# When the v of a later batch is issued, in a linear attention with routed experts behind it

## The chip, the cores and the metric

The kernel runs on one core of a Trainium2 chip. The metric is the device time of one execution in microseconds; lower is better.

## The reference

The inputs q, k and v have the shape (8 batches, 8 heads, 576 tokens, 64), all float32. The first stage is a linear attention, the second a layer of eight experts (512 to 1024 to 512, relu between them) in which a hash of the token's id names its one expert.

```python
q_s = softmax(q, axis=-1); k_s = softmax(k, axis=2)    # over features; over tokens
kv  = einsum('bhsd,bhse->bhde', k_s, v)
x   = einsum('bhsd,bhde->bhse', q_s, kv)               # then (B*S, H*D) = (4608, 512)
e   = token_ids * 2654435761 % 8
out = relu(x @ w1[e]) @ w2[e]                          # each row with its own expert
```

All of k and all of v of a batch must be there before the 64 by 64 matrices `kv` of that batch are complete.

## The kernel before

The program is written engine by engine. A small class, `Emit`, keeps a list of instructions for each engine, and in each list they run in the order in which the Python code emits them. It also works out the waits: an operation names the buffers that it reads (`R`), writes (`W`) and partly writes (`P`), and gets a wait on the semaphore of each engine or transfer that touched them before. The second argument of `em.dma` is the name of the semaphore, the first the engine on whose list the issue stands.

The attention runs over the batches b = 0 to 7, with p = b % 2 as the side of the double buffers. What one batch does:

- q and k (1.18 MB each) come from the SyncE queue, by `load_one` (L290) into `qf[p]` and `kf[p]`. `load(b + 2, p)` (L752) is emitted two batches ahead; the issue of q waits for `exp_q` of batch b (it reads the buffer), that of k for `exp_k` of batch b.
- v comes from the GpSimd queue, by `load_v` (L302), and is turned into bf16 on the way. It has four slots, `vx`, so it can be asked for early.
- ScalarE takes exponentials: `exp_k` (L517, to `ek`) and `exp_q` in two halves (L513, to `eq`).
- TensorE transposes q (`transpose_q`), and `kv(p, n)` (L542) multiplies `ek` with slot n of v: 36 matmuls at L550. `qsum` and `attend` then give the rows `xn`, by VectorE at L582.
- `sort` (L597) brings the rows of the batch before into the order of their experts by a matmul with one-hot columns (L601); ScalarE copies the result to `xs` (L608).
- `segments` (L634) copies pieces of `xs` into `xT`, the experts' input. It is a generator of 16 copies per batch (L645), eight for each of the two groups of tokens, at positions that `load_segments` has put in registers. In most batches GpSimd makes them. `run(gen, n)` (L730) takes the next n of them.

In the loop, TensorE's list for batch b is: transposes of b, first `sort` of b - 1, `kv` of b, second `sort` of b - 1, `qsum`, `attend`. ScalarE's is: `exp_k` of b, a copy of the transposed q, two copies of each `sort` to `xs`, then `exp_q` of b + 1. GpSimd's is: the issue of a v, then the copies of the segments of b - 1, which wait for both pairs of `xs`. So on GpSimd an issue of v written ahead of the copies runs as soon as the copies of the batch before are done.

The order of v before the change, in these lines: v of batches 0 and 1 at the start, of 2 in b = 0, of 3 to 6 in b = 1 to 4, and of 7 in b = 6.

```python
exp_k(p)                      # L744
transpose_q(p)
one_hot(b)
if b > 0:
    sort(1 - p, 0, 3)
...
kv(p, b % 4)                  # L753
if 0 < b < B - 1:
    sort(1 - p, 2, 0)
```

After the loop the experts follow. `l1` (matmuls at L683) and `layer2` (L708) take one expert after the other. Their weights come by the GpSimd queue, the first of them in b = 6 after the v of batch 7, into the memory that q and k leave. The rows are stored by indirect transfers (L724).

Of the kernel before, what the change touches and what calls it, by code (L numbers as in the profile page):

```python
# [164 lines left out]
def fused_kernel(nc, q, k, v, moe_token_ids, moe_w1, moe_w2, out):  # L165
    B, H, S, DH = q.shape
    NTOK = moe_token_ids.shape[0]
    E, D, F = moe_w1.shape
# [119 lines left out]
    b_q, b_k = [Buf(), Buf()], [Buf(), Buf()]  # L288
# [13 lines left out]
    def load_v(b, n, R=()):  # L302
        o = 3 * (n % 2)
        em.dma("pool", "d_v%d" % n, lambda e: e.dma_start(
            vx[n // 2][:, o:o + 2, :, :, :].rearrange("p a j c d -> p (a j) (c d)"),
            v[b].rearrange("(a h) (p c) d -> (h p) a (c d)", h=2, p=64)), R=R, W=[b_vx[n]])
# [24 lines left out]
    for h in range(2):  # L331
        for a in range(2):
# [8 lines left out]
       R=[b_tok], P=[b_ei])  # L341
# [9 lines left out]
       R=[b_ef2, bc["iota8"]], W=[b_flg])  # L351
# [5 lines left out]
          R=[b_flg, bc["upper"], bc["ones"]], W=[bk[6], bk[7]])  # L357
# [13 lines left out]
       R=[b_pr], W=[b_pos])  # L371
# [137 lines left out]
    def load(b, p):  # L509
        load_one("d_q%d", qf, q, b, p, b_q)  # L510
        load_one("d_k%d", kf, k, b, p, b_k)

    def exp_q(p, j):  # L513
        ac(lambda e: e.activation(eq[p][:, j, :, :, :].rearrange("p c a d -> p a c d"),  # L514
                                  qf[p][:, j::2, :, :], ACTF.Exp), R=[b_q[p]], W=[b_eq[p][j]])

    def exp_k(p):  # L517
        ac(lambda e: e.activation(ek[p][:].rearrange("p j c a d -> p a (j c) d"),  # L518
                                  kf[p][:].rearrange("p (a j) c d -> p a (j c) d", a=2), ACTF.Exp),
           R=[b_k[p]], W=[b_ek[p]])  # L520

    def transpose_q(p):

        def tr(e, j, c, o):
            return e.transpose(PBH[:, o:o + 128], eq[p][:, j, c, :, :].rearrange("p a d -> p (a d)"), ident[:])  # L525
        for j in range(2):
            em.op("pe", [lambda e, j=j, c=c: tr(e, j, c, 1024 * j + 128 * c) for c in range(8)],
                  R=[b_eq[p][j], bc["ident"]], W=[bk[j]])
        em.op("pe", [lambda e, j=j: tr(e, j, 8, 2048 + 128 * j) for j in range(2)], R=b_eq[p] + [bc["ident"]],
              W=[bk[2]])  # L530
        for j in range(2):
            o = qT[p][:, j, :, 0:512].rearrange("p h (c x) -> p h c x", x=64)
            i = PBH[:, 1024 * j:1024 * j + 1024].rearrange("p (c h x) -> p h c x", h=2, x=64)
            if j == 0:
                dv(lambda e, o=o, i=i: e.tensor_copy(out=o, in_=i), R=[bk[0]], W=[b_qT[p][0]])
            else:
                ac(lambda e, o=o, i=i: e.activation(o, i, ACTF.Copy), R=[bk[1]], W=[b_qT[p][1]])  # L537
        dv(lambda e: e.tensor_copy(out=qT[p][:, :, :, 512:576],
                                   in_=PBH[:, 2048:2304].rearrange("p (j h x) -> p j h x", h=2, x=64)),
           R=[bk[2]], W=[b_qT[p][2]])  # L540
# [27 lines left out]
    def qsum(p):  # L568
        em.op("pe", [lambda e, t=t, j=j, h2=h2: e.matmul(
            PB[:, 5, 8 * t + 4 * j + 2 * h2:8 * t + 4 * j + 2 * h2 + 2], qt(p, t, j, h2), pair1[:],  # L570
            start=True, stop=True) for t in range(T) for j in range(2) for h2 in range(2)],
            R=b_qT[p] + [bc["pair1"]], W=[bk[5]])
        dv(lambda e: e.reciprocal(out=rq[p][:].rearrange("p t g -> p (t g)"), in_=PB[:, 5, 0:8 * T]), R=[bk[5]],
           W=[b_rq[p]])
# [13 lines left out]
    def one_hot(b):  # L588
        p = b % 2
        for t in range(T):  # L590
            g, i = t // TG, t % TG
            dv(lambda e, g=g, i=i: e.tensor_scalar(  # L592
                out=oneh[p][g][:, i, :], in0=col16[:, 0:GW[g]], scalar1=pos[:, 2 * b + g, i:i + 1],
                scalar2=None, op0=ALU.is_equal),
               R=[b_pos, bc["col16"]], W=([b_oh[p][g]] if i == 0 else ()), P=(() if i == 0 else [b_oh[p][g]]))

    def sort(p, c0, bank):  # L597

        for g, bs in ((0, bk[bank:bank + 2]), (1, bk[bank + 2:bank + 3])):
            n = 3 - g  # L600
            em.op("pe", [lambda e, g=g, i=i, k=k, n=n: e.matmul(  # L601
                PB[:, bank + (k if g == 0 else 2), (0 if g == 0 else GW[1] * k):(GW[0] if g == 0 else GW[1] * (k + 1))],
                xn[p][:, 3 * g + i, 128 * (c0 + k):128 * (c0 + k) + 128], oneh[p][g][:, i, :],
                start=(i == 0), stop=(i == n - 1)) for k in range(2) for i in range(n)],
                R=b_xn[p][3 * g:3 * g + n] + [b_oh[p][g]], W=bs)
            src = PB[:, bank:bank + 2, 0:GW[0]] if g == 0 else \
                PB[:, bank + 2, 0:2 * GW[1]].rearrange("p (k x) -> p k x", k=2)
            ac(lambda e, g=g, src=src: e.activation(xs[p][:, c0:c0 + 2, XO[g]:XO[g] + GW[g]], src, ACTF.Copy),  # L608
               R=bs, P=b_xs[p][c0:c0 + 2])
# [24 lines left out]
    def segments(b, key="pool", half=None):  # L634
        p = b % 2
        for g in range(2):
            for ee in range(E) if half is None else range(4 * half, 4 * half + 4):
                def seg(e, ee=ee, g=g):
                    if half is None:
                        rs, o = regs[key, None, 0], 2 * E * g + 8 * (ee // 4) + ee % 4  # L640
                    else:
                        rs, o = regs[key, half, p], 8 * g + ee % 4
                    so = e.snap(rs[o], min_val=0, max_val=GW[g])  # L643
                    do = e.snap(rs[o + 4], min_val=CAPS * ee, max_val=CAPS * ee + CAP)
                    return e.tensor_copy(out=xT[:, :, bass.ds(do, SEG[g])],  # L645
                                         in_=xs[p][:, :, XO[g]:XO[g] + GW[g] + SEG[g]][:, :, bass.ds(so, SEG[g])])
                em.op(key, seg, R=b_xs[p] + ([] if b < B - 2 else [b_x5[ee]]), W=[(b_x5 if b < B - 2 else b_x7)[ee]])
                yield
# [9 lines left out]
    def weights1(ee, s, R=()):  # L658
        for a in range(2):
            em.dma("pool", "d_w1_%d" % s, lambda e, a=a: e.dma_start(  # L660
                w1b[s][64 * a:64 * a + 64, :, :],
                moe_w1[ee].rearrange("(a g p) f -> a p g f", a=2, g=4)[a]), R=R,
                W=(b_w1[s] if a == 0 else ()), P=(() if a == 0 else b_w1[s]))
# [66 lines left out]
    def run(gen, n=2 * E):  # L730
        for _ in range(n):
            if next(gen, 0) == 0:
                break
# [7 lines left out]
    for b in range(B):  # L741
        p = b % 2
        last = b == B - 1
# [5 lines that stand above are left out]
        if last:  # L749
            sort(1 - p, 2, 0)  # L750
        if b + 2 < B:
            load(b + 2, p)  # L752
# [3 lines that stand above are left out]
        if not last:  # L756
            exp_q(1 - p, 0)
            exp_q(1 - p, 1)
        qsum(p)
        if b == 0:  # L760
            load_v(2, 2)
        elif b < B - 3:
            load_v(b + 2, (b + 2) % 4)
        elif b == B - 2:
            load_v(B - 1, 3)
        if b == B - 2:
            for s, bs in enumerate(([b_q[0], b_k[0]], [b_q[1], b_k[1]])):
                b_w1[s], b_w2[s] = [Buf(*bs), Buf(*bs)], Buf(*bs)
            weights1_half(0, 0, 0)
            weights1_half(0, 0, 1)  # L770
            load_segments(b - 1, "pool")
            run(segments(b - 1))
        elif last:
            weights1(1, 1)
            weights2(0, 0)
            for x in (b - 1, b):
                load_segments(x, "pool", 1)
                load_segments(x, "dve", 0)
            run(segments(b - 1, "pool", 1))
        elif b > 0:  # L780
            load_segments(b - 1, "pool")
            run(segments(b - 1))
        attend(p, 0, 2, 3)
        attend(p, 2, 2, 6)
        attend(p, 4, 1, 5)
        if b == 0:
            segment_table()
            widths()
        if b == 1:
            overflow()  # L790
        if b == 2:
            load_widths()
# [121 lines left out]
    for b in range(B):  # L914
# [11 lines left out]
        for ch in range(4):  # L926
# [4 lines left out]
                R=b_xn[0] + [b_id], W=bk[u:u + 2])  # L931
            ac(lambda e, ch=ch, u=u: e.activation(xg[:, ch, :].rearrange("p (h x) -> p h x", h=2),
                                                  PB[:, u:u + 2, 0:H2], ACTF.Copy), R=bk[u:u + 2], W=[b_xg[ch]])
        for ee in range(E):
# [5 lines left out]
            for t in range(T):  # L940
                u = layer2(NW, t, 2)
                m = flg[:, 2 * b + t // TG, ee, t % TG:t % TG + 1]
                if ee == 0:
                    dv(lambda e, t=t, u=u, m=m: e.tensor_scalar(out=yg[:, t, :], in0=PB[:, u, :], scalar1=m,
                                                                scalar2=None, op0=ALU.mult),
                       R=[bk[u], b_flg], W=[b_yg[t]])
                else:
                    dv(lambda e, t=t, u=u, m=m: e.scalar_tensor_tensor(
                        out=yg[:, t, :], in0=PB[:, u, :], scalar=m, in1=yg[:, t, :], op0=ALU.mult, op1=ALU.add),
                       R=[bk[u], b_flg], W=[b_yg[t]])  # L950
# [39 lines left out]
```

The softmax here doesn't subtract the row's maximum and nothing guards it: scores larger than these inputs give would overflow.

## Time and profile before

| | |
|---|---|
| time | 230.05 us (median of 3 runs, 229.86 to 230.22) |
| span in the profile | 228.4 us |
| TensorE matmuls busy | 198.9 us, 87% |
| GpSimd busy | 121.6 us, 53% |
| VectorE busy | 116.1 us, 51% |
| ScalarE busy | 105.7 us, 46% |
| hardware queue (q, k) | 18.91 MB, 22.9% of the 16 DMA engines' time |
| software queue (v, weights, stores) | 30.94 MB, 67.1% |

Busy time of an engine is the sum over its instructions, and the share is of the whole span. The span falls into two parts. In the first 90 us the attention runs, with all engines busy for part of the time; from there on TensorE works on the experts almost without a pause. An average over both tells little of either, so what the change may do has to be read from the first part. In the views, a line such as L304 is a line of the kernel, and "vx<-in_v_dram" is the transfer from v in the chip's memory to the tile `vx`.

### The profile page before, as it was taken

To read this page: it belongs to the slowest core of one execution; us is meant where nothing else is said; L and a number is where in the kernel's file an instruction comes from. 1 tells how busy PE (TensorE), PEld (TensorE's weight loads), DVE (VectorE), ACT (ScalarE), POOL (GpSimd) and SP (SyncE) were. 2 spreads that over 40 slices of the span, in tenths; PEclk is the share of its full clock that TensorE was granted. 3 is DMA by queue.
4 is the path that set the end of the run, shared out by engine and by line. 5 is a ranking of instruction groups with operands and counts; after the bars stand their busy time and mean duration, and the time that the engine had idled before them with its cause. 6 is when DMAs were issued, how large, how long until landed. Compare 5 with 4: busy or idle time off the path is not lost.

```text
span 228.4 us, 4640 instructions
## 1 busy us (share of the span) xinstructions
PE 198.9 (87%) x1786; PEld 134.5 (59%) x1788; DVE 116.1 (51%) x265; ACT 105.7 (46%) x133; POOL 121.6 (53%) x235
## 2 busy tenths in 40 slices
PE   0459968876899788999999999999999999999990
PEld 0348757654776564775574764754855845845640
DVE  1678798782778867699941322322421422412220
ACT  3385588756888944765342331331422322322311
POOL 8740778773659993670007975805715615125053
PEclk9999999997999999999999999999999999999999
DMA  6999999999996999799993799999999798113023
GB/s 208 295 371 293 292 372 316 301 312 351 297 401 250 149 196 195 119 153 204 207 177 139 160 204 205 330 272 201 290 200 242 163 203 224 73 46 139 24 102 123
DMA packets 29776, 50.25 MB, mean 220 GB/s; under 512 B 2351, under 2 KB 15663, under 8 KB 29744
## 3 DMA queue, kind: packets, MB, share of 16 engines
q0 software_dynamic: 20768, 30.94, 67.1%
q1 hardware_dynamic: 8976, 18.91, 22.9%
q8 instruction: 16, 0.26, 0.4%
q14 instruction: 16, 0.13, 0.2%
HBM read 61.90 MB, written 10.49 MB: 317 GB/s over the span
## 4 chain that ended last, share of the span: by engine, by line
PE 62%; DMA 20%; POOL 6%; ACT 5%; issue 4%; POOLq 1%; DVE 1%; SPq 1%; DVEq 0%; ACTq 0%
PE ps L708 29%; PE ps L683 27%; DMA kf<-in_k_dram 20%; POOL xT L645 4%; PE ps L601 3%; ACT ek L518 3%; PE ps L550 2%; ACT eq L514 1%; POOL out_dram L724 1%; ACT xs L608 1%; PE ps L819 1%; DVE xn L582 1%; POOLq L643 1%; POOL w1b L668 0%; POOL w1b L660 0%
## 5 line engine op out<-in xcount | busy, mean ns | idle before, releaser
L724 POOL DMA_INDIRECT out_dram<-yo,idx x40 | 39.5, 987 | 71.6 <-ACT yo L718 31.8
L708 PE MATMUL ps<-w2b,hT 128*128 128x512 bf16 x320 | 70.4, 379 | 0.0
L683 PE MATMUL ps<-xT,w1b 128*128 128x320 bf16 (+1 forms) x512 | 64.4, 286 | 0.8 <-ACT hT L690 0.8
L683 PEld LDWEIGHTS ps<-xT,w1b 128*128 128x128 bf16 x512 | 49.7, 98 | 15.1 <-ACT hT L690 1.1
L708 PEld LDWEIGHTS ps<-w2b,hT 128*128 128x128 bf16 x320 | 31.2, 98 | 36.3
L645 POOL COPY xT<-xs x112 | 39.6, 412 | 19.4 <-ACT xs L608 17.9
L690 ACT ACTIVATE hT<-ps 128x640 bf16<-128x640 f32 x41 | 28.8, 703 | 39.4 <-PE ps L683 39.0
L718 ACT ACTIVATE yo<-ps 128x512 f32<-128x512 f32 x26 | 15.5, 597 | 54.1 <-PE ps L708 54.1
L692 DVE TENSOR_SCALAR hT<-ps 128x640 bf16<-128x640 f32 x23 | 19.0, 825 | 30.2 <-PE ps L683 30.2
L720 DVE COPY yo<-ps 128x512 f32<-128x512 f32 x14 | 9.7, 692 | 44.0 <-PE ps L708 44.0
L601 PE MATMUL ps<-oneh,xn 128*128 128x384 bf16 (+1 forms) x160 | 25.0, 307 | 1.3 <-ACT qT L537 1.0
L582 DVE TENSOR_TENSOR xn<-ps,rq 128x1024 bf16<-128x1024 f32 (+1 forms) x24 | 23.6, 1041 | 3.2 <-PE ps L577 2.6
L608 ACT ACTIVATE xs<-ps 128x768 bf16<-128x768 f32 (+1 forms) x32 | 19.1, 651 | 9.2 <-PE ps L601 9.1
L518 ACT ACTIVATE ek<-kf 128x2304 bf16<-128x2304 f32 x8 | 17.0, 2123 | 9.9 <-DMA kf<-in_k_dram 9.9
L550 PE MATMUL ps<-vx,ek 64*128 64x192 bf16 x288 | 15.2, 264 | 7.2 <-ACT ek L518 7.2
L601 PEld LDWEIGHTS ps<-oneh,xn 128*128 128x128 bf16 x160 | 14.8, 102 | 10.1 <-issue 2.5
L514 ACT ACTIVATE eq<-qf 128x1152 bf16<-128x1152 f32 x16 | 17.7, 1162 | 2.0 <-DMA qf<-in_q_dram 2.0
L550 PEld LDWEIGHTS ps<-vx,ek 64*128 64x128 bf16 x288 | 12.9, 102 | 9.0 <-ACT ek L518 8.5
L525 PE MATMUL ps<-ident,eq 128*128 128x128 bf16 x144 | 12.2, 244 | 5.0 <-ACT eq L514 5.0
L525 PEld LDWEIGHTS ps<-ident,eq 128*128 128x128 bf16 x144 | 10.0, 111 | 6.1 <-ACT eq L514 5.7
L592 DVE TENSOR_SCALAR oneh<-col,pos 128x384 bf16<-128x384 f16 (+1 forms) x40 | 13.5, 403 | 0.0
L674 POOL DMA_DIRECT2D w2b<-in_moe_w_dram x16 | 12.4, 798 | 0.0
(101 smaller groups left out, 131.1 us busy)
## 6 DMA issues: line engine op xcount, KB each, us to landing
qf<-in_q_dram SPq DMA_DIRECT2D x8, 1152.0 KB, 15.7
kf<-in_k_dram SPq DMA_DIRECT2D x8, 1152.0 KB, 16.9
w2b<-in_moe_w_dram POOLq DMA_DIRECT2D x16, 512.0 KB, 11.5
w1b<-in_moe_w_dram POOLq DMA_DIRECT2D x14, 512.0 KB, 9.3
vx<-in_v_dram POOLq DMA_DIRECT2D x8, 576.0 KB, 11.1
w1b<-in_moe_w_dram POOLq DMA_DIRECT2D x4, 256.0 KB, 7.8
out_dram<-yo,idx POOLq DMA_INDIRECT x40, 4.4
tok<-in_moe_token_ids_dram SPq DMA_DIRECT2D x1, 36.0 KB, 5.6
```

The source lines that it names most:

```text
L514: ac(lambda e: e.activation(eq[p][:, j, :, :, :].rearrange("p c a d -> p a c d"), qf[p][:, j::2, :, :], ACTF.Exp), R=[b_q[p]], W=[b_eq[p][j]])
L518: ac(lambda e: e.activation(ek[p][:].rearrange("p j c a d -> p a (j c) d"), kf[p][:].rearrange("p (a j) c d -> p a (j c) d", a=2), ACTF.Ex ...
L525: return e.transpose(PBH[:, o:o + 128], eq[p][:, j, c, :, :].rearrange("p a d -> p (a d)"), ident[:])
L550: fns.append(lambda e, j=j, c=c, h2=h2, r=r: e.matmul(PB[:, 6 + h2, 192 * j:192 * j + 192], ek[p][r, j, c, :, :].rearrange("p a d -> p (a ...
L582: dv(lambda e: e.tensor_tensor(out=xn[p][:, t0:t0 + n, :].rearrange("p t (g x) -> p (t g) x", x=DH), in0=PB[:, bank:bank + n, :].rearrange ...
L601: em.op("pe", [lambda e, g=g, i=i, k=k, n=n: e.matmul(PB[:, bank + (k if g == 0 else 2), (0 if g == 0 else GW[1] * k):(GW[0] if g == 0 els ...
L608: ac(lambda e, g=g, src=src: e.activation(xs[p][:, c0:c0 + 2, XO[g]:XO[g] + GW[g]], src, ACTF.Copy), R=bs, P=b_xs[p][c0:c0 + 2])
L645: return e.tensor_copy(out=xT[:, :, bass.ds(do, SEG[g])], in_=xs[p][:, :, XO[g]:XO[g] + GW[g] + SEG[g]][:, :, bass.ds(so, SEG[g])])
L683: em.op("pe", [lambda e, d=d, k=k: e.matmul(cut(PB[:, u + k, 0:H2]), w1b[s][:, d, 128 * (f + k):128 * (f + k) + 128], cut(rhs(d)), start=( ...
L690: ac(lambda e: e.activation(o, i, ACTF.Relu), R=bk[u:u + 2], W=[b_hT[hp][hf][f // 2]])
L708: em.op("pe", [lambda e, fc=fc: e.matmul(PB[:, u, :], hT[hp][:, fc, 128 * t:128 * t + 128], w2b[s][:, fc, :], start=(fc == 0), stop=(fc == ...
L724: em.dma("pool", "d_o%d" % y, lambda e: e.indirect_dma_start(out=out[:, :], out_offset=IndirectOffsetOnAxis(ap=idx[:, 5 * ee + t:5 * ee + ...
```

## The change

The change moves the issue of four of the eight v. It is for the transfers of q and k, which run on the same DMA engines as those of v: a v that is asked for later leaves the engines to the k that is wanted first.

- v of batch 2 gets a further condition, `R=[b_k[1]]`: its issue waits until k of batch 1 has landed.
- v of batch 3 stays where it was, in b = 1 ahead of the copies.
- v of batches 4, 5 and 6 (b = 2, 3, 4) moves from ahead of the copies of `segments(b - 1)` to between their two groups of eight. E is 8 in `run(sg, E)`.
- v of batch 7 stays where it was.

```diff
         if b == 0:
-            load_v(2, 2)
-        elif b < B - 3:
-            load_v(b + 2, (b + 2) % 4)
+            load_v(2, 2, R=[b_k[1]])
+        elif b == 1:
+            load_v(3, 3)
         elif b == B - 2:
             load_v(B - 1, 3)
...
         elif b > 0:
             load_segments(b - 1, "pool")
-            run(segments(b - 1))
+            sg = segments(b - 1)
+            run(sg, E)
+            if 1 < b < B - 3:
+                load_v(b + 2, (b + 2) % 4)
+            run(sg)
```

## The prediction

> **What bounds the kernel now.** I read the page first, for the chain that ended last, then that chain in order of time, then the DMA issues, the stretches of two microseconds and the timeline around the loads. The first view, part 4 of the page, gives shares of the span:
>
> ```profile
> PE 62%; DMA 20%; POOL 6%; ACT 5%; issue 4%; POOLq 1%; DVE 1%; SPq 1%; DVEq 0%; ACTq 0%
> ```
>
> PE's 62% is nearly all the expert layers after 90 us, which run without a break. What the change touches is the 20%, loads of k. In order of time (start, length, what) the chain has them like this:
>
> ```profile
> 14.38 17.04 DMA kf<-in_k_dram
> 31.44 2.13 ACT ek L518
> 33.63 17.57 DMA kf<-in_k_dram
> 51.23 2.13 ACT ek L518
> 53.40 2.21 PE ps L550 x36
> ```
>
> Up to 51.2 us the kernel is paced by the landing of k: k of batch 2 at 31.4, of batch 4 at 51.2. From there the chain is engine work until its end. So time saved before 51 us reaches the end only if no later load stops it. The stretches (window, length, busy time and count of PE, PEld, DVE, ACT, POOL, then PE clock, DMA share, GB/s) show what v does to k:
>
> ```profile
> 48.00:50.00 2.00, 1.57 (x22) 1.19 (x19) 2.00 (x4) 0.78 (x1) 2.00 (x6) 1.00 1.13 290
> 52.00:54.00 2.00, 0.60 (x16) 0.60 (x18) 0.06 (x1) 2.00 (x2) 1.27 (x4) 1.00 1.12 320
> 54.00:56.00 2.00, 2.00 (x28) 1.49 (x25) 0.31 (x2) 1.34 (x3) 0.00 (x0) 0.59 1.02 399
> 56.00:58.00 2.00, 2.00 (x13) 1.15 (x11) 0.72 (x2) 0.31 (x1) 0.00 (x0) 0.56 1.11 326
> 64.00:66.00 2.00, 2.00 (x30) 1.45 (x25) 1.31 (x4) 1.16 (x3) 0.81 (x3) 1.00 1.05 414
> ```
>
> The DMA engines are always full. Where q and k are alone they move 400 to 414 GB/s; where a v is in flight 290 (v is counted as bf16 written, half its bytes). In the trace's packet records the two queues then alternate one for one, about 85 packets each per us, against some 175 of q and k alone. A q or k has 512 large packets, so it takes 3.0 us alone; a v takes 6.1 to 7.5 us of shared time and costs the q and k beside it about 3.1. The total is fixed; order alone can change. The issue times and the two kinds of wait are in the timeline (start, length, engine, line) and in the DMA issues (last figure: us from issue to landing; here of v of batch 4 and k of batch 4):
>
> ```profile
> 36.35 0.75 POOL L304 DMA_DIRECT2D vx<-in_v_dram  x1
> 37.84 5.64 POOL L645 COPY xT<-xs  x16 [0.74 <-ACT xs L608]
> 43.42 0.74 POOL L304 DMA_DIRECT2D vx<-in_v_dram  x1
> 46.93 5.66 POOL L645 COPY xT<-xs  x16 [2.77 <-ACT xs L608]
> 52.53 0.74 POOL L304 DMA_DIRECT2D vx<-in_v_dram  x1
> ...
> 46.56 2.22 ACT L514 ACTIVATE eq<-qf 128x1152 bf16<-128x1152 f32 x2
> 51.23 2.12 ACT L518 ACTIVATE ek<-kf 128x2304 bf16<-128x2304 f32 x1 [2.45 <-DMA kf<-in_k_dram]
> ```
>
> ```profile
> kf<-in_k_dram SPq DMA_DIRECT2D x1, 1152.0 KB, 17.6
> vx<-in_v_dram POOLq DMA_DIRECT2D x1, 576.0 KB, 11.9
> ```
>
> ScalarE idles 2.45 us at 48.8 for k of batch 4; that is what can be won. v of batches 1, 3, 4, 5, 6 took 10.8, 11.8, 11.9, 10.9, 11.3 us from issue to landing, mean 11.3: by the packet records 4.1 us pass before the first packet, the rest is shared transfer. v of batch 4 landed at 48.3 and was wanted at 53.4: five microseconds of slack, and this slack is what the change spends.
>
> **What the Trainium skill says.** "DMA: Bandwidth & Descriptors", section Queues, rings and completion order, says that an engine round-robins between the queue rows it has work for, at packet granularity. The trace agrees (one for one), and within the v queue v of batch 2 begins at 22.37 just when v of batch 1 ends: first come, first served. "TensorE: Matmul & The Clock Gate", section What's actually happening, says that a free-running window of 3.4 us with too little work halves PE's clock for the next. Here the granted clock is 0.59 and 0.56 from 54 to 58 us, after a wait of 2.54 us for ek, in a window that was 28% busy by my sum of the matmul records; windows 67% busy kept the full clock. Its section Step-by-step says that matmuls stay in program order; so a kv that waits for v holds the second sort behind it, and with that the copies to xs and the exponentials of the next q on ScalarE.
>
> **The change part by part.**
>
> First, v of batch 2 behind k of batch 1. Before, both v of batches 1 and 2 are issued at 12.1 and 12.9. k of batch 1 lands at 20.2, while v of batch 1 is still running (to 22.4) and v of batch 2 stands behind it. So k of batch 1 gains nothing. GpSimd waits until 20.2, and nothing suffers: behind the wait stands the table of segments, which starts only at 23.65, after VectorE. v of batch 2 then runs from 24.3 to 30.6 instead of 22.4 to 28.8 and lands near 31.5, before its kv at about 33.4. By the packet sums k of batch 2 gains 0.3 us at most and k of batch 3 none. I take 0.
>
> Second, v of batches 4, 5, 6 between the copies. v of batch 3 stays at 28.47. The first eight copies take 2.8 us (half of 5.64). v of batch 4 goes from 36.35 to 37.84 + 2.8 = 40.65, and of batch 5 from 43.42 to 46.93 + 2.8 = 49.75. The second eight copies come 0.74 us later, hidden, since xs of that parity is written again only two batches on. The issue in itself costs nothing more: it was on GpSimd before.
>
> k of batch 4: q and k of batch 4 need 6.0 to 6.3 us alone from about 39.5. Without v they run to 44.7 (40.65 + 4.1), 5.2 us; the last 1.1 takes 2.2 shared; with about 1 us from last packet to landing, 48. ScalarE is then bound by its own work and starts ek at 48.8, not 51.23; ek is done at 50.9 and the first sort is off PE at 50.87.
>
> v of batch 4: 40.65 + 11.3 = 51.95. So kv of batch 4 starts at about 52.0 and not at 53.40: of 2.45 us, v takes back 1.1. PE's idle time before it is 1.2 us instead of 2.54, and the window stays some 65% busy: I take full clock. From kv to the copies is then 4.22 us as for batches 2 and 3 (33.62 to 37.84, 42.71 to 46.93), not the 5.73 of 53.40 to 59.13.
>
> v of batch 6: copies from 52.0 + 4.2 = 56.2, issue at 59.0, landing at 59.0 + 11.3 = 70.3.
>
> v of batch 5: 49.75 + 11.3 = 61.05. kv of batch 5 could start at 52.0 + 8.14 = 60.2 (8.14 is the full ScalarE period, 63.05 to 71.19), so it waits 0.9 and starts at 61.1 (before 63.05). kv of batch 6 could start at 61.1 + 8.14 = 69.25, but v lands at 70.3: it waits 1.1 more and starts at 70.4. Before: 71.19. Left: 0.8 us.
>
> After that nothing new is added. The v of batch 7 is issued after the copies of batch 4, some 1.6 us earlier; k of batch 7 lands at 73.7 as before (total fixed) and is wanted at 76.4. From exponentials of batch 7 to the first expert layer, and from there to the end, everything shifts with kv of batch 6, since PE has no gap after 92 us and the weights, too, start 1.6 us earlier. So 230.05 - 0.75 = 229.3.
>
> **The rivals.**
>
> A, v comes sooner. If v lands in 10.8 us as for batch 1, kv of batch 4 starts at 51.4, v of batch 6 lands at 69.2. But k of batch 6 must land too, and its place is after 14 pieces of q and k and six v; I get 67.4, hence kv at 67.4 + 2.2 = 69.6. The gain ends at 1.6 us: 228.4. For it: three of five v had 11.3 or less. Against: the mean is what three v in a row should average to, and the DMA engines stay as full as now.
>
> B, v comes later, at 11.9 as for batch 4: kv of batch 4 at 52.6, copies 56.8, issue 59.6, landing 71.5, kv of batch 6 at 71.55. The wait for v takes all that k gave: no change, 230.1 (230.4 by the sum).
>
> C, slower. The wait for v at 52.0 still halves the clock: 5.73 instead of 4.22 us puts v of batch 6 at 71.8, kv at 71.9, a loss of 0.7: 230.75. With late v as well, 232. For it: the chain runs through two landings of v, and each later v issue hangs on the kv before. Against: a 1.2 us gap leaves any window mostly busy.
>
> D, k and v hide behind each other with full gain (2.45 us plus the clock, to 227): excluded by k of batch 6 above; I give it 3%.
>
> **How the numbers follow.** Forecast 0.42, A 0.22, B 0.17, C 0.16, D 0.03. The forecast is 229.3, with 229.59 the bound of faster by 0.2% (0.46 us). Of the forecast's own spread (two landings, each about 0.4 us off, so 0.6 together) three quarters lies below that bound: faster 0.32 + 0.22 + 0.03 = 0.57. Same: 0.10 + 0.14 = 0.24. Slower: 0.16 + 0.03 = 0.19. The range reaches from a little beyond A, 228.2, to C, 230.8.
>
> **What would show it.** Right: ek of batch 4 starting near 48.8 with no wait for k; PE waiting for v (named as DMA vx) before kv of batches 4, 5, 6; v issues at 40.7, 49.8, 59.0; clock 1.00 from 54 to 58; kv of batch 6 near 70.4. Wrong: kv of batches 4 to 6 released by ek, that is v early (A or D); or clock near 0.5 after 54 us (C); or k of batch 1 landing before 19.5, which would mean that the two early v did share.

## The result and the profile after

| | before | after |
|---|---|---|
| time | 230.06 us (229.86 to 230.22) | 231.71 us (231.57 to 235.46) |
| ratio, 95% interval | | 1.007 [1.005, 1.009] |
| span in the profile | 228.4 us | 230.0 us |
| kv of batch 6 starts | 71.19 us | 72.60 us |

The change makes the kernel 0.7% slower, 1.65 us by the medians; 229.3 was forecast. Executions over 1.5% longer than the shortest of their kernel are left out of the ratios here and below, but not out of the medians and ranges.

The chain that ended last has changed its middle. In order of time (start, length, what; PE, DVE, ACT, POOL and SP are TensorE, VectorE, ScalarE, GpSimd and SyncE), after:

```profile
14.55 16.66 DMA kf<-in_k_dram
...
41.91 11.38 DMA vx<-in_v_dram
53.43 1.66 PE ps L550 x36
...
60.86 11.60 DMA vx<-in_v_dram
72.60 1.66 PE ps L550 x36
```

Before, the landing of k of batch 4 at 51.2 stood here, and kv of batches 5 and 6 followed without a wait, 8.14 us apart (before, timeline of TensorE):

```profile
63.05 1.66 PE L550 MATMUL ps<-vx,ek 64*128 64x192 bf16 x36
...
71.19 1.66 PE L550 MATMUL ps<-vx,ek 64*128 64x192 bf16 x36
```

Now two transfers of v stand in it one behind the other, those of batches 4 and 6. Between them lies work that depends on the first: kv of batch 4, the second sort, the copies to xs, eight copies of segments, and only then the second issue. The timeline after, for GpSimd, ScalarE and TensorE (start, length, engine, line, and in brackets the idle time before and what ended it):

```profile
38.72 3.24 POOL L645 COPY xT<-xs  x8 [2.48 <-ACT xs L608]
41.91 0.75 POOL L304 DMA_DIRECT2D vx<-in_v_dram  x1
50.41 0.74 POOL L304 DMA_DIRECT2D vx<-in_v_dram  x1
60.86 0.74 POOL L304 DMA_DIRECT2D vx<-in_v_dram  x1
...
48.95 2.12 ACT L518 ACTIVATE ek<-kf 128x2304 bf16<-128x2304 f32 x1
...
33.41 1.80 PE L550 MATMUL ps<-vx,ek 64*128 64x192 bf16 x36 [1.97 <-ACT ek L518]
35.14 2.74 PE L601 MATMUL ps<-oneh,xn 128*128 128x384 bf16 x10
53.43 1.66 PE L550 MATMUL ps<-vx,ek 64*128 64x192 bf16 x36 [2.27 <-DMA vx<-in_v_dram]
62.36 1.66 PE L550 MATMUL ps<-vx,ek 64*128 64x192 bf16 x36 [0.76 <-DMA vx<-in_v_dram]
72.60 1.66 PE L550 MATMUL ps<-vx,ek 64*128 64x192 bf16 x36 [2.07 <-DMA vx<-in_v_dram]
```

The aim was reached: ek of batch 4 starts at 48.95 with no wait for k (before: 51.23, after 2.45 us of idle time). But kv of batch 4 then waits 2.27 us for v and starts at 53.43, when it had started at 53.40. Nothing of the 2.3 us is left, and v of batch 6 still has its 11.6 us to come.

Two lines were not foreseen. The eight copies take 3.2 us from the first to the issue. And the sort at 35.14 takes 2.74 us, not 1.48: PE ran at half clock, as the stretches after show (the third figure from the right is the PE clock):

```profile
34.00:36.00 2.00, 2.00 (x29) 1.27 (x26) 0.96 (x4) 1.35 (x3) 2.00 (x8) 0.70 1.19 240
36.00:38.00 2.00, 2.00 (x19) 1.39 (x18) 0.34 (x1) 0.72 (x2) 0.24 (x1) 0.50 1.06 388
54.00:56.00 2.00, 2.00 (x34) 1.47 (x29) 0.80 (x3) 0.00 (x0) 0.00 (x0) 1.00 1.11 320
```

There is one more. SyncE's issues after: the issue of k of batch 3, the second line, was at 22.39 before.

```profile
18.00 0.37 SPq L291 DMA_DIRECT2D qf<-in_q_dram  x1
32.27 0.37 SPq L291 DMA_DIRECT2D kf<-in_k_dram  x1
```

`R=[b_k[1]]` does two things. It makes the issue of v wait for k, and it enters the transfer of v as a reader of that buffer. The next writer, k of batch 3, then waits for v of batch 2 to land, at 32.2 us. The prediction missed this wait altogether.

### The profile page after: what moved, and what is told of

It reads as the page before. It is cut to its first block, busy times and chain, and to the rows that moved or that the text cites. A ratio compares the mean times of both kernels' runs of the same rounds, so it can differ in the third digit from the quotient of the medians.

```text
span 230.0 us, 4641 instructions
## 1 busy us (share of the span) xinstructions
PE 196.7 (86%) x1786; PEld 132.5 (58%) x1788; DVE 115.9 (50%) x265; ACT 105.4 (46%) x133; POOL 122.1 (53%) x235
## 4 chain that ended last, share of the span: by engine, by line
PE 63%; DMA 22%; DVE 4%; ACT 3%; issue 3%; POOL 2%; DVEq 1%; SPq 1%; POOLq 0%; ACTq 0%
PE ps L708 29%; PE ps L683 26%; DMA kf<-in_k_dram 12%; DMA vx<-in_v_dram 10%; PE ps L601 4%; PE ps L550 3%; DVE xn L582 2%; ACT ek L518 2%; POOL xT L645 1%; DVEq L631 1%; ACT xs L608 1%; POOL out_dram L724 1%; PE ps L823 1%; DVE oneh L592 1%; POOLq L643 0%
## 5 line engine op out<-in xcount | busy, mean ns | idle before, releaser
L724 POOL DMA_INDIRECT out_dram<-yo,idx x40 | 39.5, 988 | 71.6 <-ACT yo L718 31.8
L708 PE MATMUL ps<-w2b,hT 128*128 128x512 bf16 x320 | 70.4, 379 | 0.0
L550 PEld LDWEIGHTS ps<-vx,ek 64*128 64x128 bf16 x288 | 12.6, 100 | 11.8 <-ACT ek L518 6.6
L525 PE MATMUL ps<-ident,eq 128*128 128x128 bf16 x144 | 11.2, 232 | 4.9 <-ACT eq L514 4.9
L525 PEld LDWEIGHTS ps<-ident,eq 128*128 128x128 bf16 x144 | 9.1, 104 | 5.9 <-ACT eq L514 5.6
```

The lines of the kernel that those rows point to most:

```text
L550: fns.append(lambda e, j=j, c=c, h2=h2, r=r: e.matmul(PB[:, 6 + h2, 192 * j:192 * j + 192], ek[p][r, j, c, :, :].rearrange("p a d -> p (a ...
L708: em.op("pe", [lambda e, fc=fc: e.matmul(PB[:, u, :], hT[hp][:, fc, 128 * t:128 * t + 128], w2b[s][:, fc, :], start=(fc == 0), stop=(fc == ...
L724: em.dma("pool", "d_o%d" % y, lambda e: e.indirect_dma_start(out=out[:, :], out_offset=IndirectOffsetOnAxis(ap=idx[:, 5 * ee + t:5 * ee + ...
```

## The experiments

Three theories. T1: the two landings of v set the time. T2: gaps before kv let the PE clock fall to half in some executions. T3: the hidden wait of k of batch 3 costs. kv(6) is the start of kv of batch 6 in the run's own trace, which is one execution; times are medians. "Half clock" names windows of 3.41 us that the trace's clock records have at half speed between 23 and 90 us. The runs came in four groups on three chips; "before" is the median of the kernel before in the same group, and each ratio is to that.

**Each part alone, and the hidden wait taken out.**

```diff
# p1_only: before, with part one
-            load_v(2, 2)
+            load_v(2, 2, R=[b_k[1]])
# p2_only: after, without part one
-            load_v(2, 2, R=[b_k[1]])
+            load_v(2, 2)
# no_read: after, the same wait on a copy of the record, so no reader is entered
-            load_v(2, 2, R=[b_k[1]])
+            load_v(2, 2, R=[Buf(b_k[1])])
```

p1_only: 

> The first part alone: v of batch 2 behind the landing of k of batch 1, all other v as before. T1: 230.0 to 230.2, no change. T3: k of batch 3 is issued near 32 us; if that costs, 230.4 to 231.5, with exponentials of k of batch 3 waiting longer than before.

p2_only: 

> The second part alone: v of batch 2 is issued at once, v of batches 4 to 6 between the copies. Theory T1 (two landings of v, of batches 4 and 6, set the time, part one is idle): as the whole change, 231.5 to 231.8. Theory T3 (the read that part one registers on the buffer of k holds the issue of k of batch 3 from 22.4 to 32.3 us and what follows): better than the whole change, 230.4 to 230.8, with k of batch 3 issued near 22.4. T2 (phase of the PE clock): anything between 230.4 and 231.8, by whether a window at half clock lies before 38 us.

no_read: 

> The whole change, with the same wait for k of batch 1, but without the read registered on its buffer, so that k of batch 3 need not wait for v of batch 2. T1: 231.5 to 231.8 as the whole change, though k of batch 3 is issued near 22.4. T3: 230.4 to 230.8.

| run | time | before | ratio, 95% interval | kv(6) | half clock at |
|---|---|---|---|---|---|
| p1_only | 230.64 | 229.78 | 1.0019 [0.9996, 1.0041] | 71.39 | 54.6 |
| p2_only | 234.94 | 229.78 | 1.0198 [1.0140, 1.0255] | 76.16 | 34.5, 54.9, 75.4 |
| no_read | 230.95 | 229.78 | 1.0065 [1.0044, 1.0086] | 71.76 | none |

Part one alone makes no difference that can be told. Its median lies in T3's range and above T1's, but its executions fall into two groups (five from 228.9 to 229.6, nine from 230.2 to 230.95), those of before spread as widely (228.8 to 230.5), and the interval contains 1; a loss of up to 0.4% isn't excluded by this run. The exponentials of k of batch 3 waited 0.91 us in its trace, against 0.84 before, where T3 wanted a longer wait.

The test of T3 is no_read. There k of batch 3 is issued at 22.58 again, and the ratio is that of the whole change (1.0065 against 1.007, and 1.0061 in after_again below): T3 falls. The time itself, 230.95, lies between the two ranges that were set from the first pair. The reason can be read from the packets: while k of batch 3 was held, v of batch 3 had the DMA engines nearly for itself (from 33 to 36 us in the trace after, 445 of 549 packets), and exponentials of k of batch 3 began at 40.72 after and 40.64 in no_read. p2_only fits no expectation in size; it has three windows at half clock, so it was run again below.

**The place of v between the copies.**

```diff
# after_one: after the first copy; after_six: after the sixth
-            run(sg, E)
+            run(sg, 1)
```

after_one: 

> The whole change, but v of batches 4 to 6 after the first copy of 16 instead of after the eighth, 2.8 us earlier at each. T1: the waits of kv for v go from 2.3, 0.8 and 2.1 us to 0, kv of batch 6 near 68 to 69.6, time 228.2 to 229. T3 alone: the time stays at 231 or above.

after_six: 

> The whole change, but v of batches 4 to 6 after the sixth copy instead of the eighth, 0.8 us earlier at each of the two issues that count. T1: kv of batch 6 earlier by 1.6, 1.0 to 1.6 us less than the whole change on this chip: 229.2 to 230. A theory in which only the number of v in flight counts, not when they land, has no change from eight to six.

after_again: 

> The whole change again, on the chip and beside the runs of before of the next three. Theory T1 (two landings of v in a row set kv of batch 6: first copy of the segments + 3.2 + 11.4, then 4.2 + 3.2 + 11.6 us): 230.5 to 231.7, with kv of batches 4 and 6 waiting for v. Theory T2 (the gaps before kv let the PE clock fall to half, by the phase of its window): single executions up to 4 us longer, the shortest near 230.5.

| copies ahead of v | time | before | ratio, 95% interval | kv(6) |
|---|---|---|---|---|
| 1 (after_one) | 228.81 | 229.78 | 0.9961 [0.9949, 0.9973] | 69.80 |
| 6 (after_six) | 229.62 | 229.39 | 1.0017 [0.9998, 1.0037] | 70.24 |
| 8 (after_again) | 230.97 | 229.39 | 1.0061 [1.0034, 1.0088] | 71.25 |

This is the test that carries T1: the time follows the moment of the issue. From eight to six copies it falls by 1.35 us, inside the 1.0 to 1.6 foreseen. The trace of after_six, though, gets there by another v: kv of batch 4 waits for none, kv of batch 5 waits 1.85 us for its own v (issued at 50.21) and starts at 62.10, and kv of batch 6 follows 8.14 us later without a wait. (This trace has half clock from 15.6 to 22.5 and at 39.5, the other two have none after 23 us.) With one copy v is in time and another limit comes up. The timeline of after_one, TensorE and ScalarE:

```profile
69.80 1.66 PE L550 MATMUL ps<-vx,ek 64*128 64x192 bf16 x36 [0.73 <-ACT ek L518]
...
67.62 2.12 ACT L518 ACTIVATE ek<-kf 128x2304 bf16<-128x2304 f32 x1 [0.64 <-DMA kf<-in_k_dram]
```

kv of batch 6 is released by ek, and ek by k, which lands at 67.6: the limit that the prediction's rival A had put at 67.4, with kv at 69.6.

The trace of after_again has no half clock, so it shows the whole change without that. Timeline, GpSimd and TensorE:

```profile
37.35 3.23 POOL L645 COPY xT<-xs  x8 [0.68 <-ACT xs L608]
40.54 0.75 POOL L304 DMA_DIRECT2D vx<-in_v_dram  x1
56.34 3.26 POOL L645 COPY xT<-xs  x8 [2.81 <-ACT xs L608]
59.54 0.74 POOL L304 DMA_DIRECT2D vx<-in_v_dram  x1
...
52.11 1.66 PE L550 MATMUL ps<-vx,ek 64*128 64x192 bf16 x36 [1.06 <-DMA vx<-in_v_dram]
71.25 1.66 PE L550 MATMUL ps<-vx,ek 64*128 64x192 bf16 x36 [0.79 <-DMA vx<-in_v_dram]
```

The steps are those of the prediction, but 40.54 to 52.11 and 59.54 to 71.25 are 11.6 and 11.7 us, and 37.35 to 40.54 and 56.34 to 59.54 are 3.2. kv of batch 5 came late too, at 62.29: its v, issued at 50.31, took 11.8 us.

**Which of the moved v.**

```diff
# v4_only: v of batch 4 alone between the copies (v6_only: that of batch 6, b == B - 4)
-        elif b == 1:
-            load_v(3, 3)
+        elif b < B - 3 and b != 2:
+            load_v(b + 2, (b + 2) % 4)
...
-            if 1 < b < B - 3:
+            if b == 2:
```

v4_only: 

> Of the moved v only that of batch 4 stands between the copies, v of batches 5 and 6 ahead of them as before; v of batch 2 as in the change. T1: k of batch 4 is early, kv of batch 4 waits for v until about 52.4, kv of batch 6 is not held by v and starts near 70.4; 228.9 to 229.4. T2: as before, since the same gap stands before kv of batch 4.

v6_only: 

> Of the moved v only that of batch 6 stands between the copies; v of batches 4 and 5 ahead of them as before, v of batch 2 as in the change. Theory T1 (two landings of v in a row set the time): k of batch 4 is as late as before, near 51, kv of batch 4 near 53.3, then 4.2 + 3.2 + 11.6 us to kv of batch 6 near 72.4: 231 to 231.8, no better than the whole change. A theory in which the move of v of batch 4 does the harm: 229.4 or less.

v4_only takes 229.28 us (before: 229.39), 0.9989 [0.9969, 1.0008]. This time is in T1's range and is also that of before, so the time doesn't part T1 from T2; the trace does (TensorE):

```profile
52.58 1.66 PE L550 MATMUL ps<-vx,ek 64*128 64x192 bf16 x36 [1.73 <-DMA vx<-in_v_dram]
69.60 1.66 PE L550 MATMUL ps<-vx,ek 64*128 64x192 bf16 x36
```

kv of batch 4 still waits 1.73 us for v, but no second landing follows. v6_only takes 235.1 us (before: 229.43), 1.0259 [1.0216, 1.0302], far above the 231.8 that T1 allowed. Its kv(6), 72.88, is near the 72.4 foreseen; TensorE's timeline and the stretches show what came on top:

```profile
72.88 2.73 PE L550 MATMUL ps<-vx,ek 64*128 64x192 bf16 x36 [3.09 <-DMA vx<-in_v_dram]
75.55 2.03 PE L601 MATMUL ps<-oneh,xn 128*128 128x384 bf16 x10
```

```profile
74.00:76.00 2.00, 2.00 (x23) 1.52 (x19) 0.32 (x2) 0.00 (x0) 0.97 (x2) 0.50 1.12 184
```

The 3.09 us for v emptied a window, and the next ran at half clock: kv 2.73 us instead of 1.66, the sort 2.03 instead of 1.48. From kv to the next ek it took 7.6 us (72.88 to 80.47), not 5.96. This trace is of the shortest of the four executions, 233.6 us; what the other three, up to 235.9, lost beyond that wasn't traced.

**The clock.**

```diff
# fill: after; before_fill: before
+        if b in (2, 4, 5, 6):
+            em.op("pe", [lambda e: e.transpose(PBH[:, 6912:7040], ident[:], ident[:])] * 12,
+                  R=[bc["ident"]], W=[bk[6]])
         kv(p, b % 4)
```

p2_again: 

> The second part alone, a second time. T1: as the whole change, 230.5 to 231.7 in most executions; the first result, 232.9 to 236.4, then came from windows at half clock in those executions (T2) and a trace without such windows has kv of batch 6 near 71.8. T3 (the wait on v of batch 2 that k of batch 3 got with part one is what costs): 230.0 or less.

fill: 

> The whole change with 12 more transposes of the unit matrix, which nothing reads, ahead of kv of batches 2, 4, 5 and 6; they only raise the share of busy time of TensorE in the windows that have the gaps. Theory T2 (half clock after gaps makes the long executions and part of the median): no window at half clock between 25 and 90 us, the executions above 232 gone, median 230.2 to 230.6. T1 alone: kv of batch 6 near 71.3 as in the trace without a half-clock window, and median not below 230.2, since the landings of v stay. If the clock plays no part: 231.0, with the long executions still there.

fill_again: 

> The whole change with the 12 more transposes, again, beside the kernel before with the same transposes. If two landings of v alone make the loss, the clock apart: 1.2 to 1.6 us longer than that one, and no execution above 232.

before_fill: 

> The kernel before with 12 more transposes ahead of kv of batches 2, 4, 5 and 6. If the window at half clock after the wait for k of batch 4 made the longer half of its executions (229.9 to 230.6): all of them at 228.8 to 229.5, and kv of batch 6 near 70.3. If the clock plays no part in before: as before, or 0.1 longer.

| run | time | before | ratio, 95% interval | executions from, to |
|---|---|---|---|---|
| after_again | 230.97 | 229.39 | 1.0061 [1.0034, 1.0088] | 230.24, 235.60 (10) |
| p2_again | 234.63 | 229.39 | 1.0114 [1.0050, 1.0178] | 231.10, 350.17 (6) |
| fill | 230.75 | 229.43 | 1.0052 [1.0035, 1.0070] | 230.27, 231.56 (13) |
| fill_again | 230.70 | 229.53 | 1.0056 [1.0039, 1.0073] | 229.93, 232.60 (22) |
| before_fill | 230.18 | 229.53 | 1.0026 [1.0010, 1.0041] | 229.73, 231.26 (22) |

p2_again had two executions of 231.1 and 231.4, as T1 has it, and three of 234.5 to 235.4, where T1 had expected most below 231.7; its ratio rests on 231.10, 231.43 and 234.47. The trace (span 233.0 us) has half clock at 35.0, 55.5 and 75.9. T3 is excluded again, since none came near 230.0. One execution of 350 us, at a mean clock of 0.58, is left aside.

So part two alone is longer than the whole change: seven of these nine executions lie at 232.9 or more, against five of 33 of after, after_again and no_read. Part one makes no difference alone; beside part two, by these runs, it does. The traces show what goes ahead of the first half clock. In p2_only, p2_again, after and before_third the clock records have full clock from 17.4 to 18.2 us on, kv of batch 1 starts at 23.3, kv of batch 2 waits 1.97 to 2.31 us for ek, and half clock follows at 34.5 to 35.3. In the other ten traces without the added transposes below, kv of batch 1 starts at 24.3 to 24.9, that wait is 0.4 to 1.2 us, and no half clock follows there. Why part two alone falls into the first group so often stays open.

With the added transposes the longest executions are gone: none of 35 lies above 232.6, where four of 33 without them lie above 233. That points to half clock as what makes the tail, as the traces of long executions do (p2_only, p2_again, v6_only). The median hardly moves, by 0.2 to 0.3 us, and fill's 230.75 is a little above the 230.2 to 230.6 that T2 wanted; a window at half clock at 40.2 was still there in its trace. In the trace of fill_again there is none, and kv(6) starts at 71.36, near the 71.3 of T1.

Two expectations failed. before_fill is not faster: the transposes cost 0.6 us ahead of each kv that waits for nothing (ek to kv 2.81 instead of 2.18 at batch 5). fill_again is 0.5 us longer than before_fill, not 1.2 to 1.6, and two of its executions lie above 232. The cost of the transposes in before_fill is the likely reason for the first, but this wasn't tested apart. So the fill runs don't give the clock's share in the medians, and that in before is taken from two more traces.

**The base.**

before_again: 

> The kernel before, for a second trace. With a window at half clock after 50 us: kv of batch 6 near 71.2 and a span near 228.4. Without one: kv of batch 6 near 70.3 and a span near 227.5.

before_third: 

> The kernel before, for a third trace, with the same two cases.

The timeline of before_again, TensorE, and two stretches:

```profile
53.96 1.66 PE L550 MATMUL ps<-vx,ek 64*128 64x192 bf16 x36 [2.05 <-ACT ek L518]
70.24 1.66 PE L550 MATMUL ps<-vx,ek 64*128 64x192 bf16 x36
```

```profile
54.00:56.00 2.00, 2.00 (x39) 1.70 (x40) 0.31 (x2) 1.90 (x3) 0.33 (x1) 1.00 1.04 403
56.00:58.00 2.00, 2.00 (x41) 1.76 (x39) 1.13 (x3) 1.26 (x3) 0.00 (x0) 1.00 1.05 396
```

kv of batch 4 is later than in the first trace of before (53.96 against 53.40), kv(6) 0.95 us earlier, because the clock stayed whole after it: 229.26 us. In this trace kv(6) comes 16.28 us after kv of batch 4, twice the 8.14; in the first trace it came 17.79 us after. before_third has kv(6) at 69.86 and 229.05 us, though with half clock at 35.3; there k of batch 4 also came sooner (ek at 49.93 after 0.15 us of waiting), so its early kv(6) isn't the clock's doing alone. The trace that the prediction argued from was thus one of the longer executions of before.

**A better version.**

```diff
# no_read_one: after with both edits; one_fill: with the transposes of fill as well
-            load_v(2, 2, R=[b_k[1]])
+            load_v(2, 2, R=[Buf(b_k[1])])
...
-            run(sg, E)
+            run(sg, 1)
```

no_read_one: 

> v of batches 4 to 6 after the first copy, and no read registered on the buffer of k of batch 1, so that k of batch 3 is issued near 22.4. T1: bound by the landing of k, as after one copy alone: 228.4 to 228.9. T3 (k of batch 3 held until 32.3 us costs DMA time that later k need): 0.3 to 0.8 us less than after one copy, 228.0 to 228.4.

one_fill: 

> The same with the 12 more transposes ahead of kv of batches 2, 4, 5 and 6. If windows at half clock still cost where v is early: 0.2 to 0.5 us less than without them. If k sets the time: the same, or 0.1 to 0.5 more where the transposes come between k and kv.

no_read_one takes 228.70 us, 0.9966 [0.9951, 0.9981], and one_fill 228.78 us, 0.9972 [0.9957, 0.9987] (before: 229.43 for both): the same as after_one within what these tell apart. T3 fails here too. The move of v is worth 0.6 to 1.0 us if it is made early enough. How much of that is the earlier k and how much the clock wasn't parted: kv(6) in after_one is 0.4 us earlier than in before_again and about as early as in before_third (69.86), while the executions of after_one keep between 228.4 and 229.3 where those of before go up to 230.5.

## Why the prediction was wrong

Right: k of batch 4 ahead of ScalarE (48 foreseen, no wait measured at 48.95); PE waiting for v before kv of batches 4, 5 and 6; the chain through two landings of v; no gain from part one that could be told (alone; beside part two it counted, as p2_only and p2_again show); the limit of 69.6 for kv(6) through k of batch 6. One statement in it was wrong without consequence: "nothing suffers" from the wait for k of batch 1, where k of batch 3 was held for 10 us.

Wrong was the sum for kv of batch 6, 70.4, against 72.60 in the profile after, and the 71.19 it was held against. The path through the two landings of v was the right one; its terms were too short, and the base was too late. The terms:

- "The first eight copies take 2.8 us (half of 5.64)." Measured 3.2 to the issue, in each of the two rounds: 0.8 us together. The first eight of before's own trace show it (37.84 to the ninth at 41.01); half of sixteen hides it, because the first copies start every 0.40 us and the last every 0.30.
- The landing, "11.3", and what follows: 11.38 and 11.60, with 0.14 from each landing to kv: 0.5 us together.
- "I take full clock": true after kv of batch 4, but not before. The gap of 1.97 us ahead of kv of batch 2 brought half clock at 34.8, and the copies started at 38.72 instead of 37.84: 0.9 us. after_again has none of this and starts kv(6) at 71.25.
- "Before: 71.19": in before without half clock after 50 us, 70.24 and 69.86. The base was 1.0 to 1.3 us later than in these two. This alone is more than the 0.75 us of gain that was forecast. The prediction saw the half clock at 54 us and its cost (5.73 instead of 4.22), and yet took 71.19 as what before always does.

The first, second and last turn the forecast gain into a loss of about 1 us with the clock whole after 23 us on both sides, after_again against before_again: 71.25 against 70.24. (The first two add 1.3 us to 70.4; the chain of after_again began 0.5 us earlier than foreseen, at 37.35.) The loss arises between kv of batch 4 and kv of batch 6: 16.28 us in before_again, 19.14 in after_again, 19.17 in after. That is rival B's wait with more on it. Rival C foresaw the direction and some of the size, but by half clock behind the wait at 52.0, and there the clock stayed whole, in after and in after_again. The first pair of kernels differed by 0.7%, after_again and its before by 0.6%; their intervals overlap, and why three executions of the first lay at 231.6 to 231.8 is not settled beyond the half clock seen in one of them.

## What to carry over

A transfer moved behind the work that it is to make room for gets into a chain with itself when that work waits for the transfer before it: here the issue of v of batch 6 hung on a kv that hung on v of batch 4, and every tenth of a microsecond in the steps counted twice. Move it only as far as its slack, and take the slack from the first instruction to the issue, not from a mean over a group. And before a forecast of less than 1% is made from one trace, look for what in that trace is chance.

## What was not expected of the hardware

- Whether a gap costs 1 us more or nothing depends on where the clock's windows lie: in before the wait of 2.54 us was followed by half clock in one trace, and one of 2.05 us in another was not. The page of the Trainium skill that the prediction cites for the clock ("TensorE: Matmul & The Clock Gate", What's actually happening) has half clock after an idle window; here windows that were partly busy were enough. By the sum of matmul records, one 42% busy was followed by half clock (31.4 to 34.8 after) and one 47% busy was not (68.9 to 72.3 after). Over the 18 traces, between 23 and 90 us, all twelve windows at full clock that were 42% busy or less were followed by half clock, and of 331 that were 46% busy or more only one, at 57% (36.1 to 39.5 in after_six).
- Half clock came three times in p2_only and in p2_again, each 20.5 us after the last, which is six windows: kv of batches 2, 4 and 6 started 20.4 and 20.3 us apart in p2_again, so there the gap met the same place of the window each time.
- v from issue to first packet takes 4.1 us whether GpSimd goes on with copies at once (41.91 to 46.00 after) or rests (28.47 to 32.58 before). v of batch 7, issued when the DMA engines were nearly idle (a share of 0.01 from 73 to 74 us before), took 1.4 us (73.16 to 74.61 before).
